# Window attention, forward and backward: six 64-row products per window pair as four 64 by 64 tiles of the PE array, with compact probabilities and a new step order

## Chip, cores, metric

One NeuronCore of one Trainium2 chip. The metric is device time of one execution in microseconds (us). PE is the engine of the matrix products, DVE the vector engine, ACT the scalar engine.

## The reference

The input is a 256 x 256 image of 384 channels, cut into 1024 windows of 8 x 8 = 64 tokens. Each window has single-head attention over its own tokens; the kernel computes the output and the gradients of x, wqkv and wo.

```python
qkv = xw @ wqkv                                  # xw: (1024, 64, 384)
p = softmax(einsum('bqc,bkc->bqk', q, k) * C ** -0.5)
o = einsum('bqk,bkc->bqc', p, v) @ wo
# ... and the vector-Jacobian product of all of it with grad_out
```

## The kernel before

Weights are multiplied together first, so that per token only projections by four 384 x 384 matrices remain. One body of the main loop handles four window pairs ("quad", t = 0..3); a pair fills the 128 partitions with two windows of 64 tokens. The body runs 128 times. Per pair, six products of the 64 x 64 probability matrix P, or of its gradient S, with token tensors of 384 columns are needed: the output, two inputs of the weight gradients (U, W), and three that accumulate into the gradient of x. P and S of the two windows stood on the diagonal of 128 x 128 matrices that were zeroed once, so that each product was one full-array product, half of it zeros.

```python
# softmax, step 3 (step 5 is alike for pd and S): one DVE operation per window, 64 partitions each
for w, h in halves:
    nc.vector.tensor_tensor(out=Pb[h, :, h], in0=ex[h, :, :], in1=ri[h, :]..., op=ALU.mult)

def turn(st, kind):            # PT, ST: 128 x 128 transposes, 512-column copy
    for t in range(QUAD):
        nc.tensor.transpose(pt[:, t, :], src[:, t, :], ident[:])
    nc.vector.tensor_copy(out=dst[:], in_=pt[:])

def attend(st, t, part):       # one 128-row product per part, three in part 3; ps_at has 2 buffers
    if part == 0:    matmul(pa, lhsT=PT[:, t, :], rhs=uq[:, t, :]);  ACT copies to osb; DMA out
    elif part == 1:  matmul(pa, lhsT=Pb[:, t, :], rhs=dq[:, t, :]);  DVE copies to Wq
    elif part == 2:  matmul(pa, lhsT=ST[:, t, :], rhs=xq[:, t, :]);  ACT copies to Uq
    else:            # Pb*zq + Sb*yq + ST*vq;                        ACT copies to dsb; DMA out

def step(a, b):                # a: this quad, b: the one before it
    A(project, 0, 0); B(0, 0); A(project, 0, 1); B(0, 1); A(project, 0, 2); B(0, 2); ...  # parts one by one
    filler(4); A(scores); A(soft, 0); ...
    # ... [cut: soft 1 to 5 between uv products and the other parts of B]
    for t in range(QUAD):
        A(yz_tok, t, 0); filler(2); A(yz_tok, t, 1); filler(2)   # token transposes, DVE copies yq, zq
    A(turn, 1); filler(2)
```

In the names, xq and dq are the tokens of x and grad_out; uq and vq are x times two of the four matrices, yq and zq the transposed projections by the other two. The softmax goes through mx (maximum), sh (shifted scores), ex, rs and ri (sum and its reciprocal) to P; pr, D and pd lead on to S.

A filler is one 384-column product of the weight gradient; twelve make a group, which DVE then adds to GF_acc. PE, DVE and ACT run in the order written here.

## Time and profile before

| | before |
|---|---|
| time, median of three runs | 2829.28 us (2827.99 to 2836.85) |
| mean body, from the first to the last score maximum | 21.54 us |
| PE / DVE / ACT busy | 88% / 70% / 49% |
| projections to scores ("stage 1"), softmax ("stage 2"), token transposes ("stage 3") of the body below | 6.68 / 10.13 / 4.69 us |

The page of the profile gives the busy time of each engine. PE records overlap, so 88% does not mean that the array streams for 88% of the time.

```profile
span 2827.3 us, 50549 instructions
PE 2485.4 (88%) x18814; PEld 1474.1 (52%) x18814; DVE 1976.6 (70%) x4899; ACT 1379.3 (49%) x2957; POOL 549.2 (19%) x1036
```

The chain of waits of the kernel before, one body. Columns: start (us), share of the chain (us), engine, output and line, number of instructions.

```profile
1422.04 0.65 PE pj L147 x3
1422.69 0.16 PE pa L243
...
1427.94 0.76 PE sd L161 x24
1428.70 0.02 issue
1428.72 0.43 DVE mx L174
...
1432.96 0.42 DVE P_bd_233 L192
1433.38 0.03 issue
1433.41 0.43 DVE P_bd_233 L192
...
1437.49 0.56 DVE Wq L249
1438.05 0.33 DVE PT L233
...
1438.85 0.28 DVE yq L225
...
1443.54 0.65 PE pj L147 x3
```

From 1422.04 to the first score maximum (mx, 1428.72) the chain lies on PE. From there to the first token copy (yq, 1438.85) it lies on DVE but for one visit to PE of 0.7 us. From there to the next body's first projection (1443.54) it is mostly on PE again. These three stretches are the stages of this text. Two groups of instructions that the change replaces (busy us, mean ns of one; then idle time before them):

```profile
L248 PE MATMUL pa<-dq,P_bd_225 128*128 128x384 bf16 x172 | 56.1, 326 | 0.0
L192 DVE TENSOR_TENSOR P_bd_225<-ex,ri 64x256 bf16<-64x256 f32 x86 | 36.1, 420 | 2.9
```

There is such a group for each of the three block-diagonal buffers.

### The profile page before, as it was taken

The numbers are of one execution on the slowest core, as the hardware profiler recorded it, in microseconds if no ns is written. First come the engines' busy times: TensorE is split into PE (matmuls) and PEld (weight loads), VectorE is DVE, ScalarE is ACT, GpSimd is POOL, SyncE is SP. The second block draws the span as 40 slices with busy tenths as digits, with TensorE's granted clock in tenths as the row PEclk, the third lists the DMA queues.
The fourth block names the chain that finished last, engine by engine and source line by source line (L and its number), as shares of the span: only waits on it lengthen the run. The fifth ranks groups of instructions, "written<-read, shape, count | busy, mean of one in ns | idle before, by whom it ended". The sixth has DMA issues, their size and how long they took to land.

```text
span 2827.3 us, 50549 instructions
## 1 busy us (share of the span) xinstructions
PE 2485.4 (88%) x18814; PEld 1474.1 (52%) x18814; DVE 1976.6 (70%) x4899; ACT 1379.3 (49%) x2957; POOL 549.2 (19%) x1036
## 2 busy tenths in 40 slices
PE   6888988888898888889888988888898888889887
PEld 3455555555555555555555555555555555555554
DVE  5677677767767776776777677677767776776774
ACT  3554554455455445545544554554454445545552
POOL 2121122112111211211221121112111211221110
PEclk9999999999999999999999999999999999999999
DMA  6444444455444444445554444444445544444441
GB/s 154 92 112 103 110 106 110 111 115 122 113 110 106 111 103 110 112 105 116 117 118 107 111 108 107 107 108 108 106 116 113 122 109 111 106 110 105 110 93 41
DMA packets 599863, 307.74 MB, mean 109 GB/s; under 512 B 434240, under 2 KB 582464, under 8 KB 599616
## 3 DMA queue, kind: packets, MB, share of 16 engines
q1 hardware_dynamic: 550064, 203.49, 34.2%
q0 software_dynamic: 49152, 100.73, 12.9%
q8 instruction: 147, 2.41, 0.3%
q14 instruction: 100, 0.82, 0.1%
q10 hardware_dynamic: 400, 0.29, 0.0%
HBM read 101.84 MB, written 101.84 MB: 72 GB/s over the span
## 4 chain that ended last, share of the span: by engine, by line
PE 51%; DVE 43%; issue 3%; DMA 2%; ACT 1%; SPq 0%; ACTq 0%; DVEq 0%
PE pj L147 18%; PE pw L271 13%; DVE uq L218 9%; PE pt L224 5%; DVE sh L180 4%; DVE mx L174 4%; PE pj L216 3%; PE sd L161 3%; DVE pr L197 3%; DVE pd L204 3%; DVE yq L225 3%; DVE GF_acc L274 3%; DVE Wq L249 2%; DVE D L199 2%; DMA out_dram<-osb 2%
## 5 line engine op out<-in xcount | busy, mean ns | idle before, releaser
L259 POOL DMA_DIRECT2D out_dram<-dsb x512 | 275.3, 538 | 2205.6 <-ACT dsb L258 2170.9
L150 ACT CAST yz<-pj 128x512 bf16<-128x512 f32 x384 | 227.1, 592 | 843.1 <-PE pj L147 843.1
L216 PEld LDWEIGHTS <-xT 128*128 128x128 bf16 x3072 | 299.2, 97 | 368.8 <-issue 200.4
L249 DVE CAST Wq<-pa 128x384 bf16<-128x384 f32 x512 | 283.4, 554 | 272.8 <-PE pa L248 268.8
L216 PE MATMUL pj<-B_sb,xT 128*128 128x384 bf16 x1536 | 333.3, 325 | 98.9 <-ACT vq L218 72.6
L271 PE MATMUL pw<-Wq,xq 128*128 128x384 bf16 x1536 | 364.2, 326 | 47.6 <-DVE GF_acc L274 47.6
L252 ACT CAST Uq<-pa 128x384 bf16<-128x384 f32 x512 | 245.7, 480 | 315.3 <-PE pa L251 315.3
L271 PE MATMUL pw<-Uq,xq 128*128 128x384 bf16 x1536 | 359.9, 326 | 24.9 <-DVE GF_acc L274 24.9
L216 PE MATMUL pj<-AT_sb,xT 128*128 128x384 bf16 x1536 | 334.6, 327 | 35.3 <-DVE uq L218 35.3
L271 PEld LDWEIGHTS <-xq 128*128 128x128 bf16 x3072 | 258.5, 98 | 142.3 <-issue 89.9
L147 PE MATMUL pj<-dT,BT_sb 128*128 128x512 bf16 x1152 | 316.0, 384 | 6.2 <-DMA dT<-dq 6.2
L218 DVE CAST uq<-pj 128x384 bf16<-128x384 f32 x512 | 284.5, 556 | 43.5 <-PE pj L216 35.5
L147 PE MATMUL pj<-xT,A_sb 128*128 128x512 bf16 x1152 | 311.3, 379 | 0.0
L245 ACT CAST osb<-pa 128x384 bf16<-128x384 f32 x512 | 246.8, 482 | 92.3 <-DMA out_dram<-osb 52.2
L258 ACT CAST dsb<-pa 128x384 bf16<-128x384 f32 x512 | 244.9, 478 | 73.5 <-PE pa L256 61.1
L132 POOL DMA_DIRECT2D dq<-in_grad_out_dram x512 | 270.6, 542 | 37.8 <-PE pt L232 26.1
L218 ACT CAST vq<-pj 128x384 bf16<-128x384 f32 x512 | 244.0, 477 | 57.2 <-PE pj L216 54.7
L224 PE MATMUL pt<-ident,zc 128*128 128x128 bf16 x1536 | 169.9, 220 | 95.5 <-DVE PT L233 94.8
L225 DVE COPY yq<-pt 128x384 bf16<-128x384 bf16 x512 | 182.1, 356 | 102.6 <-PE pt L224 85.3
L153 ACT CAST yz<-pj 128x512 bf16<-128x512 f32 x384 | 229.9, 599 | 16.4 <-PE pj L147 0.7
L151 DVE COPY zc<-yz 128x512 bf16<-128x512 bf16 x384 | 112.9, 294 | 177.8 <-ACT yz L150 177.7
L224 PEld LDWEIGHTS <-zc 128*128 128x128 bf16 x1536 | 129.1, 98 | 178.7 <-issue 121.3
(107 smaller groups left out, 3558.8 us busy)
## 6 DMA issues: line engine op xcount, KB each, us to landing
xq<-in_x_dram SPq DMA_DIRECT2D x512, 96.0 KB, 2.5
dq<-in_grad_out_dram POOLq DMA_DIRECT2D x512, 96.0 KB, 2.5
out_dram<-osb SPq DMA_DIRECT2D x512, 96.0 KB, 2.2
out_dram<-dsb POOLq DMA_DIRECT2D x512, 96.0 KB, 2.1
xT<-xq SPq DMA_TRANSPOSE x128, 4.7
dT<-dq SPq DMA_TRANSPOSE x128, 3.7
w_sb<-in_wqkv_dram SPq DMA_DIRECT2D x1, 864.0 KB, 5.7
out_dram<-dw_sb SPq DMA_DIRECT2D x1, 864.0 KB, 3.8
```

Of the source, the lines that this page charges most:

```text
L132: nc.gpsimd.dma_start(out=dq[:, t, :], in_=dram_tile(grad_out, bp, t0 + t))
L147: nc.tensor.matmul(pj[:].rearrange("p t w k -> p (t w k)"), lhsT=wgt[:, m, mo * P:(mo + 1) * P], rhs=src[:, :, m, :], start=(m == 0), stop ...
L216: nc.tensor.matmul(pj[:], lhsT=st["xT"][:, t, m, :], rhs=wgt[:, m, :], start=(m == 0), stop=(m == CK - 1))
L218: cp(out=dst[:, t, :], in_=pj[:])
L224: nc.tensor.transpose(pt[:, m, :], src[:, m, :, :].rearrange("p w k -> p (w k)"), ident[:])
L225: nc.vector.tensor_copy(out=dst[:, t, :].rearrange("p (m c) -> p m c", m=CK), in_=pt[:])
L245: nc.scalar.copy(out=osb[:], in_=pa[:])
L249: nc.vector.tensor_copy(out=st["Wq"][:, t, :], in_=pa[:])
L252: nc.scalar.copy(out=st["Uq"][:, t, :], in_=pa[:])
L258: nc.scalar.copy(out=dsb[:], in_=pa[:])
L259: nc.gpsimd.dma_start(out=dram_tile(out_1, bp, t0 + t), in_=dsb[:])
L271: nc.tensor.matmul(pw[:], lhsT=st["xq"][:, t, ma * P:(ma + 1) * P], rhs=st["UW"[f] + "q"][:, t, :], start=(i == 0), stop=(i == n - 1))
```

## The change

Intent: use the array's four 64 x 64 quadrants for four products of 64 rows at once. Two products are issued together, one placed "straight" (rows low to low, high to high) and one "crossed", so that the four tiles never write the same PSUM partitions of the same bank. P and S are then stored compactly, 64 columns instead of 128, which also makes one DVE operation out of two. All attention of a pair is issued in one piece, four PSUM buffers hold its results, the transposes share the two buffers of the projections, and the step order is new.

```diff
-            for w, h in halves:
-                nc.vector.tensor_tensor(out=Pb[h, :, h], in0=ex[h, :, :], in1=ri[h, :]..., op=ALU.mult)
+            nc.vector.tensor_tensor(out=Pb[:], in0=ex[:], in1=over_k(ri[:]), op=ALU.mult)
 # ... [cut: the same for pd and S]
+            for h in (LO, HI):
+                nc.tensor.transpose(pt[h, t, :], src[h, t, :], ident[h, h])
 # ... [cut]
+        def both(straight, crossed):
+            for h, o, (dst, lhs, rhs, first, last) in ((LO, LO, straight), (LO, HI, crossed), (HI, LO, crossed),
+                                                       (HI, HI, straight)):
+                nc.tensor.matmul(dst[o, :], lhsT=st[lhs][h, t, :], rhs=st[rhs][h, t, :], start=first, stop=last)
+        both((po, "PT", "uq", True, True), (pd, "Pb", "zq", True, False))
+        ...                                                # ACT copies po
+        both((pu, "ST", "xq", True, True), (pd, "Sb", "yq", False, False))
+        both((pw, "Pb", "dq", True, True), (pd, "ST", "vq", False, True))
+        ...                                                # DVE copies pw, ACT copies pu and pd
 # ... [cut] the new order of one body:
+        A(project, 0, 0); A(project, 0, 1); B(0); A(project, 0, 2); A(project, 1, 0); B(1)
+        A(project, 1, 1); A(project, 1, 2); filler(8); A(scores); A(soft, 0); A(soft, 1); filler(4)
+        A(uv, 0, 0); A(uv, 0, 1); A(soft, 2); A(uv, 1, 0); A(uv, 1, 1); A(soft, 3); B(2)
+        A(uv, 2, 0); A(uv, 2, 1); A(soft, 4); A(uv, 3, 0); A(uv, 3, 1); filler(4); A(soft, 5)
+        for t in range(QUAD): A(yz_tok, t, 0); filler(1); A(yz_tok, t, 1); filler(1)
+        B(3); A(turn, 0); A(turn, 1)
```

More of the change, by code (lines that the diff above doesn't have):

```diff
@@ L60 @@
     ps_pj = ctx.enter_context(tc.tile_pool(name="ps_pj", bufs=2, space=bass.MemoryType.PSUM))
-    ps_tr = ctx.enter_context(tc.tile_pool(name="ps_tr", bufs=2, space=bass.MemoryType.PSUM))
     ps_sd = ctx.enter_context(tc.tile_pool(name="ps_sd", bufs=1, space=bass.MemoryType.PSUM))
-    ps_at = ctx.enter_context(tc.tile_pool(name="ps_at", bufs=2, space=bass.MemoryType.PSUM))
+    ps_at = ctx.enter_context(tc.tile_pool(name="ps_at", bufs=4, space=bass.MemoryType.PSUM))
     ps_dw = ctx.enter_context(tc.tile_pool(name="ps_dw", bufs=1, space=bass.MemoryType.PSUM))
@@ L75 @@
     for jm in range(JK):
-        pt = ps_tr.tile([P, C], BF16, tag="tr")
+        pt = ps_pj.tile([P, C], BF16, tag="pj")
         for m in range(CK):
@@ L81 @@
     for mo in range(CK):
-        pt = ps_tr.tile([P, C], BF16, tag="tr")
+        pt = ps_pj.tile([P, C], BF16, tag="pj")
         for m in range(CK):
@@ L108 @@
     nc.vector.memset(GF_acc[:], 0.0)
-    NBD = 3
-    P_bds = []
-    S_bds = []
-    for i in range(NBD):
-        pb = const.tile([P, QUAD, P], BF16, name=f"P_bd{i}")
-        nc.gpsimd.memset(pb[:], 0.0)
-        P_bds.append(pb)
-        sb = const.tile([P, QUAD, P], BF16, name=f"S_bd{i}")
-        nc.gpsimd.memset(sb[:], 0.0)
-        S_bds.append(sb)
     def dram_tile(ap, bp, t):
         return ap[0, 2 * WIN * bp:2 * WIN * (bp + 1), WIN * t:WIN * (t + 1), :]
-    halves = ((0, slice(0, WT)), (1, slice(WT, P)))
+    LO, HI = slice(0, WT), slice(WT, P)
     def load(st):
         bp, t0 = st["at"]
-        st["xq"] = xq = grp.tile([P, QUAD, C], BF16, tag="xq", name="xq", bufs=2 * GQ + 2)
+        st["xq"] = xq = grp.tile([P, QUAD, C], BF16, tag="xq", name="xq", bufs=2 * GQ + 3)
         st["dq"] = dq = qp.tile([P, QUAD, C], BF16, tag="dq", name="dq", bufs=4)
@@ L164, in scores, with over_k @@
                                      start=(m == 0), stop=(m == CK - 1))
+    def over_k(ap, n=P):
+        return ap.unsqueeze(2).broadcast_to([n, QUAD, WT])
     def soft(st, step):
@@ L168, in soft @@
         if step == 0:
-            st["Pb"] = P_bds[st["i"] % NBD]
-            st["Sb"] = S_bds[st["i"] % NBD]
             st["mx"] = mx = sm.tile([P, QUAD], F32, tag="mx", name="mx")
-            for w, h in halves:
-                o = slice(WT, P) if w == 0 else slice(0, WT)
-                nc.vector.tensor_reduce(out=mx[o, :], in_=sd[o, :, w, :], axis=AX.X, op=ALU.max)
+            for w, h in ((0, HI), (1, LO)):
+                nc.vector.tensor_reduce(out=mx[h, :], in_=sd[h, :, w, :], axis=AX.X, op=ALU.max)
         elif step == 1:
@@ L177, in soft @@
             st["sh"] = sh = sm.tile([P, QUAD, WT], F32, tag="sh", name="sh")
-            for w, h in halves:
-                o = slice(WT, P) if w == 0 else slice(0, WT)
-                nc.vector.tensor_tensor(out=sh[h, :, :], in0=sd[o, :, w, :],
-                                        in1=mx[o, :].unsqueeze(2).broadcast_to([WT, QUAD, WT]), op=ALU.subtract)
+            for w, h, o in ((0, HI, LO), (1, LO, HI)):
+                nc.vector.tensor_tensor(out=sh[o, :, :], in0=sd[h, :, w, :], in1=over_k(mx[h, :], WT),
+                                        op=ALU.subtract)
         elif step == 2:
@@ L185, in soft @@
         elif step == 3:
-            ex, Pb = st["ex"], st["Pb"]
+            ex = st["ex"]
             rs = sm.tile([P, QUAD], F32, tag="rs")
@@ L190, in soft @@
             nc.vector.reciprocal(out=ri[:], in_=rs[:])
-            for w, h in halves:
-                nc.vector.tensor_tensor(out=Pb[h, :, h], in0=ex[h, :, :],
-                                        in1=ri[h, :].unsqueeze(2).broadcast_to([WT, QUAD, WT]), op=ALU.mult)
+            st["Pb"] = Pb = qp.tile([P, QUAD, WT], BF16, tag="Pb", name="Pb")
+            nc.vector.tensor_tensor(out=Pb[:], in0=ex[:], in1=over_k(ri[:]), op=ALU.mult)
         elif step == 4:
             st["pr"] = pr = sm.tile([P, QUAD, WT], F32, tag="pr", name="pr")
-            for w, h in halves:
-                nc.vector.tensor_tensor(out=pr[h, :, :], in0=sd[h, :, w, :], in1=st["Pb"][h, :, h], op=ALU.mult)
+            for w, h in ((0, LO), (1, HI)):
+                nc.vector.tensor_tensor(out=pr[h, :, :], in0=sd[h, :, w, :], in1=st["Pb"][h, :, :], op=ALU.mult)
             st["D"] = D = sm.tile([P, QUAD], F32, tag="D", name="D")
@@ L200, in soft @@
         else:
-            Pb, Sb, D, pr = st["Pb"], st["Sb"], st["D"], st["pr"]
             pd = sm.tile([P, QUAD, WT], F32, tag="pd")
-            for w, h in halves:
-                nc.vector.tensor_tensor(out=pd[h, :, :], in0=Pb[h, :, h],
-                                        in1=D[h, :].unsqueeze(2).broadcast_to([WT, QUAD, WT]), op=ALU.mult)
-            for w, h in halves:
-                nc.vector.tensor_tensor(out=Sb[h, :, h], in0=pr[h, :, :], in1=pd[h, :, :], op=ALU.subtract)
+            nc.vector.tensor_tensor(out=pd[:], in0=st["Pb"][:], in1=over_k(st["D"][:]), op=ALU.mult)
+            st["Sb"] = Sb = qp.tile([P, QUAD, WT], BF16, tag="Sb", name="Sb")
+            nc.vector.tensor_tensor(out=Sb[:], in0=st["pr"][:], in1=pd[:], op=ALU.subtract)
     def uv(st, t, part):
@@ L221, in yz_tok @@
         src, dst = ((st["yz"][:, :, t, 1:3, :], st["yq"]), (st["zc"][:, :, t, :, :], st["zq"]))[part]
-        pt = ps_tr.tile([P, CK, P], BF16, tag="tr")
+        pt = ps_pj.tile([P, CK, P], BF16, tag="pj")
         for m in range(CK):
@@ L228, in turn @@
         src, n = ((st["Pb"], "PT"), (st["Sb"], "ST"))[kind]
-        st[n] = dst = qp.tile([P, QUAD, P], BF16, tag=n, name=n)
-        pt = ps_tr.tile([P, QUAD, P], BF16, tag="tr")
+        st[n] = dst = qp.tile([P, QUAD, WT], BF16, tag=n, name=n)
+        pt = ps_pj.tile([P, QUAD, WT], BF16, tag="pj")
         for t in range(QUAD):
-            nc.tensor.transpose(pt[:, t, :], src[:, t, :], ident[:])
+            for h in (LO, HI):
+                nc.tensor.transpose(pt[h, t, :], src[h, t, :], ident[h, h])
@@ L233, in turn, with attend @@
         nc.vector.tensor_copy(out=dst[:], in_=pt[:])
-    def attend(st, t, part):
+    def attend(st, t):
         bp, t0 = st["at"]
-        if t == 0 and part == 0:
+        if t == 0:
             st["Uq"] = grp.tile([P, QUAD, C], BF16, tag="Uq", name="Uq")
             st["Wq"] = grp.tile([P, QUAD, C], BF16, tag="Wq", name="Wq")
-        Pb, Sb, PT, ST = st["Pb"], st["Sb"], st["PT"], st["ST"]
-        pa = ps_at.tile([P, C], F32, tag="at")
-        if part == 0:
-            nc.tensor.matmul(pa[:], lhsT=PT[:, t, :], rhs=st["uq"][:, t, :], start=True, stop=True)
-            osb = ob.tile([P, C], BF16, tag="o")
-            nc.scalar.copy(out=osb[:], in_=pa[:])
-            nc.sync.dma_start(out=dram_tile(out_0, bp, t0 + t), in_=osb[:])
-        elif part == 1:
-            nc.tensor.matmul(pa[:], lhsT=Pb[:, t, :], rhs=st["dq"][:, t, :], start=True, stop=True)
-            nc.vector.tensor_copy(out=st["Wq"][:, t, :], in_=pa[:])
-        elif part == 2:
-            nc.tensor.matmul(pa[:], lhsT=ST[:, t, :], rhs=st["xq"][:, t, :], start=True, stop=True)
-            nc.scalar.copy(out=st["Uq"][:, t, :], in_=pa[:])
-        else:
-            nc.tensor.matmul(pa[:], lhsT=Pb[:, t, :], rhs=st["zq"][:, t, :], start=True, stop=False)
-            nc.tensor.matmul(pa[:], lhsT=Sb[:, t, :], rhs=st["yq"][:, t, :], start=False, stop=False)
-            nc.tensor.matmul(pa[:], lhsT=ST[:, t, :], rhs=st["vq"][:, t, :], start=False, stop=True)
-            dsb = ob.tile([P, C], BF16, tag="d")
-            nc.scalar.copy(out=dsb[:], in_=pa[:])
-            nc.gpsimd.dma_start(out=dram_tile(out_1, bp, t0 + t), in_=dsb[:])
@@ new lines, in attend @@
+        po = ps_at.tile([P, C], F32, tag="at", name="po")
+        pd = ps_at.tile([P, C], F32, tag="at", name="pd")
+        pu = ps_at.tile([P, C], F32, tag="at", name="pu")
+        pw = ps_at.tile([P, C], F32, tag="at", name="pw")
+        def both(straight, crossed):
+            for h, o, (dst, lhs, rhs, first, last) in ((LO, LO, straight), (LO, HI, crossed), (HI, LO, crossed),
+                                                       (HI, HI, straight)):
+                nc.tensor.matmul(dst[o, :], lhsT=st[lhs][h, t, :], rhs=st[rhs][h, t, :], start=first, stop=last)
@@ new lines, in attend @@
+        both((po, "PT", "uq", True, True), (pd, "Pb", "zq", True, False))
+        osb = ob.tile([P, C], BF16, tag="o")
+        nc.scalar.copy(out=osb[:], in_=po[:])
+        nc.sync.dma_start(out=dram_tile(out_0, bp, t0 + t), in_=osb[:])
+        both((pu, "ST", "xq", True, True), (pd, "Sb", "yq", False, False))
+        nc.scalar.copy(out=st["Uq"][:, t, :], in_=pu[:])
+        both((pw, "Pb", "dq", True, True), (pd, "ST", "vq", False, True))
+        nc.vector.tensor_copy(out=st["Wq"][:, t, :], in_=pw[:])
@@ L261 @@
+        dsb = ob.tile([P, C], BF16, tag="d")
+        nc.scalar.copy(out=dsb[:], in_=pd[:])
+        for h, w in ((LO, 1), (HI, 0)):
+            nc.gpsimd.dma_start(out=dram_tile(out_1, bp, t0 + t)[WIN * w:WIN * (w + 1)], in_=dsb[h, :])
     fill = []
@@ L290, in step @@
         A = (lambda f, *r: f(a, *r)) if a is not None else (lambda f, *r: None)
-        B = (lambda t, p: attend(b, t, p)) if b is not None else (lambda t, p: None)
+        B = (lambda t: attend(b, t)) if b is not None else (lambda t: None)
         A(project, 0, 0)
-        B(0, 0)
         A(project, 0, 1)
-        B(0, 1)
+        B(0)
         A(project, 0, 2)
-        B(0, 2)
         A(project, 1, 0)
-        B(0, 3)
+        B(1)
         A(project, 1, 1)
-        B(1, 0)
         A(project, 1, 2)
-        B(1, 1)
-        filler(4)
+        filler(8)
         A(scores)
         A(soft, 0)
-        B(1, 2)
-        filler(2)
-        B(1, 3)
         A(soft, 1)
+        filler(4)
         A(uv, 0, 0)
-        B(2, 0)
+        A(uv, 0, 1)
         A(soft, 2)
-        A(uv, 0, 1)
-        B(2, 1)
         A(uv, 1, 0)
+        A(uv, 1, 1)
         A(soft, 3)
-        B(2, 2)
-        A(uv, 1, 1)
-        B(2, 3)
+        B(2)
+        A(uv, 2, 0)
+        A(uv, 2, 1)
         A(soft, 4)
-        A(uv, 2, 0)
-        B(3, 0)
-        A(uv, 2, 1)
+        A(uv, 3, 0)
+        A(uv, 3, 1)
+        filler(4)
         A(soft, 5)
-        B(3, 1)
-        A(turn, 0)
-        A(uv, 3, 0)
-        B(3, 2)
-        A(uv, 3, 1)
-        B(3, 3)
         for t in range(QUAD):
             A(yz_tok, t, 0)
-            filler(2)
+            filler(1)
             A(yz_tok, t, 1)
-            filler(2)
+            filler(1)
+        B(3)
+        A(turn, 0)
         A(turn, 1)
-        filler(2)
     quads = [(bp, t0) for bp in range(NBP) for t0 in range(0, NT, QUAD)]
@@ L363 @@
         for mb in range(CK):
-            pt = ps_tr.tile([P, C], BF16, tag="tr")
+            pt = ps_pj.tile([P, C], BF16, tag="pj")
             for ma in range(CK):
```

## The prediction

> **What bounds the kernel now.** The loop body (four window pairs) runs 128 times; in the chain of waits two bodies follow each other at 1400.4 and 1422.0 us, a period of 21.6 us. The page gives PE 88%, DVE 70%, ACT 49%, but PE's records overlap: in the timeline products follow each other every 0.163 us (384 columns) or 0.216 us (512), so PE streams about 18 us per body. The chain of waits shows three stages. (1) Projection to scores, 6.8 us, PE-bound. (2) Softmax and its gradient, 10.0 to 10.1 us: from 1428.7 to 1438.8 us the chain lies on DVE almost without a gap. (3) Token transposes with fillers, 4.7 us, PE-bound. A faster PE alone would not shorten stage 2.
>
> **What the change does, per body.**
> - PE: 24 attention products (3.9 us) become 48 of 64x64x384. If four tiles run at once, that is 12 slots, about 2.0 us. The Trainium skill ("TensorE: Matmul & The Clock Gate", Part 3) says that packed tiles start about 4 ns apart; it says ("TensorEngine Tiling (Array Packing)", Tiling Modes) that a change of tiling mode drains the array. Four tiled sections mean eight changes; estimated from the 0.16 us by which a recorded 384-column product (0.327 us) outlasts its spacing, 1.2 to 1.6 us. So about 0.8 to 0.95 us per pair instead of 0.98: most of the PE gain is given back. The doubled transposes may cost 0.3 to 0.6 us more.
> - DVE: P, pd and S become one 128x256 operation each in place of two of 64x256 (0.42 us each): -1.26 us. PT and ST copies: -0.35 us. Together -1.6 of 15.4.
> - Moved: out of stage 2 go one Wq copy (0.55) and PT; a GF_acc addition (0.55) always falls into it. Eight fillers move before the scores, eight of the sixteen stay among the transposes, whose two PSUM buffers are now the projections'.
>
> **On the critical path, by stage** (my estimate). (1) 3.9 us projections + 1.7 tiled attention + 1.3 fillers + 0.76 scores + 0.2 = 7.9 to 8.1 us (ACT needs nearly the same). (2) DVE: 8.1 us against 10.05. (3) With fewer fillers the eight copies and their two-buffer handshake set the pace: 3.2 us, then GF_acc, Wq, PT and the last attention 1.5 to 1.6 us. Sum 20.7 to 21.0 against 21.6. So the gain comes mainly from DVE, not from the array: 0.6 to 1.2 us x 128 = 80 to 150 us.
>
> **Prediction: 2715 us, range 2600 to 2840; faster by over 2%: 0.70, within 2%: 0.18, slower: 0.12.**
>
> **What would show each step right or wrong.** P, pd, S groups each 128 records of 128x256 at about 0.42 us, DVE busy about 1780 us. Tiled products starting in near-simultaneous fours, groups 0.16 to 0.22 us apart; a gap of 0.1 to 0.2 us at each change between full and tiled. Stage 2 near 8 us on DVE; stage 3 on DVE rather than PE; stage 1 a microsecond longer. GF_acc no longer holding up PE's fillers (72 us before), ACT's osb no longer waiting for DMA.
>
> **What would make it wrong.** Tiles of one row half running one after another (group 0.33 us): pair 1.3 us, the stages on PE grow by 1.5 us, time 2800 to 2900. All four in turn: over 3000. Slow 64-column weight loads (over 50 ns, in series): the last transposes delay the next body. Cheap drains would bring 2620.

## The result, and the profile after

| | before | after |
|---|---|---|
| median (four runs each) | 2830.05 us | 2574.93 us (2573.89 to 2576.12) |
| ratio of fast runs | | 0.9095 (0.9079 to 0.9111) |
| mean body | 21.54 us | 19.64 us |
| stage 1 / 2 / 3 of one body | 6.68 / 10.13 / 4.69 us | 7.52 / 7.94 / 4.20 us |

All ratios here are the mean time of one kernel's fast runs over that of the other's of the same rounds, so not quite the ratio of the medians quoted. The time fell by 255 us; the prediction had 114 and a range that ended at 2600. The direction was right, the size was not.

```profile
span 2574.3 us, 59437 instructions
PE 2318.2 (90%) x22910; PEld 1259.7 (49%) x22910; DVE 1751.3 (68%) x4515; ACT 1295.4 (50%) x2957; POOL 862.0 (33%) x1542
```

The chain of waits of the kernel after, from one score maximum to the next (stage 2, stage 3, then stage 1 of the next body):

```profile
1401.19 0.43 DVE mx L162
...
1405.16 0.42 DVE Pb L179
1405.59 0.47 DVE Wq L241
...
1409.13 0.28 DVE yq L208
...
1412.06 0.46 DVE GF_acc L260
1412.52 0.55 DVE Wq L241
1413.08 0.21 DVE PT L217
1413.29 0.04 issue
1413.33 1.46 PE pj L135 x6
1414.78 0.28 PE po L232
...
1415.07 0.15 PE pu L232
...
1415.39 1.40 PE pj L135 x6
...
1418.81 1.30 PE pw L257 x8
1420.11 0.71 PE sd L149 x24
1420.82 0.02 issue
1420.85 0.43 DVE mx L162
```

Stage 2 is 2.2 us shorter and still on DVE. Stage 1 is 0.8 us longer: it now has twelve attention products and eight fillers where it had eight and four. A whole attention pair takes 0.61 us there (1414.78 to 1415.39), and the six projection products that follow take 1.40 us, where the same six without a change of mode (from full-array products to tiles or back) before them take 1.29 (in a run below). The groups that answer to those above:

```profile
L232 PE MATMUL pw<-dq,Pb 64*64 64x384 bf16 x1024 | 170.7, 323 | 0.0
L179 DVE TENSOR_TENSOR Pb<-ex,ri 128x256 bf16<-128x256 f32 x128 | 54.3, 424 | 4.4
```

Four tiles do run at once. PE's timeline of the kernel after, one attention pair between two full-array products:

```profile
1404.41 0.32 PE L199 MATMUL pj<-AT_sb,xT 128*128 128x384 bf16 x1
1404.66 0.35 PE L232 MATMUL po<-uq,PT 64*64 64x384 bf16 x1
1404.67 0.35 PE L232 MATMUL pd<-zq,Pb 64*64 64x384 bf16 x2
1404.67 0.35 PE L232 MATMUL po<-uq,PT 64*64 64x384 bf16 x1
1404.85 0.32 PE L232 MATMUL pu<-xq,ST 64*64 64x384 bf16 x1
...
1405.01 0.32 PE L232 MATMUL pw<-dq,Pb 64*64 64x384 bf16 x1
...
1405.28 0.34 PE L199 MATMUL pj<-B_sb,xT 128*128 128x384 bf16 x1
```

The four starts of a group lie within 0.01 us, as the Trainium skill has it ("TensorE: Matmul & The Clock Gate", Part 3: about 4 ns per tile). The groups follow each other after 0.16 to 0.19 us. Full-array products of 384 columns follow each other after 0.163 us, so the first tile starts 0.09 us late (0.25 after the product before it), and the next full product 0.11 us late (0.27 after the last group).

### The profile page after: what moved, and what is told of

It is laid out like the page before. It is cut to its first block, busy times and chain, and to the rows that moved or that the text cites. A ratio compares the mean times of both kernels' runs of the same rounds, so it can differ in the third digit from the quotient of the medians.

```text
span 2574.3 us, 59437 instructions
## 1 busy us (share of the span) xinstructions
PE 2318.2 (90%) x22910; PEld 1259.7 (49%) x22910; DVE 1751.3 (68%) x4515; ACT 1295.4 (50%) x2957; POOL 862.0 (33%) x1542
## 3 DMA queue, kind: packets, MB, share of 16 engines
q8 instruction: 179, 2.93, 0.5%
## 4 chain that ended last, share of the span: by engine, by line
DVE 49%; PE 47%; issue 2%; ACT 0%; DMA 0%; SPq 0%; ACTq 0%
PE pj L135 21%; DVE uq L201 10%; PE pw L257 10%; PE pt L207 6%; DVE GF_acc L260 5%; DVE Wq L241 5%; DVE sh L167 4%; DVE mx L162 4%; DVE pr L183 4%; PE sd L149 4%; DVE yq L208 3%; PE po L232 3%; DVE Sb L190 2%; DVE Pb L179 2%; DVE D L185 2%
## 5 line engine op out<-in xcount | busy, mean ns | idle before, releaser
L245 POOL DMA_DIRECT2D out_dram<-dsb x1024 | 586.4, 577 | 1056.1 <-ACT dsb L243 1032.0
L236 ACT CAST osb<-po 128x384 bf16<-128x384 f32 x512 | 255.0, 498 | 508.2 <-PE po L232 500.2
L135 PE MATMUL pj<-dT,BT_sb 128*128 128x512 bf16 x1152 | 293.4, 381 | 80.2 <-DVE PT L217 79.9
L257 PEld LDWEIGHTS <-xq 128*128 128x128 bf16 x3072 | 291.0, 98 | 137.2 <-issue 6.3
L162 DVE TENSOR_REDUCE mx<-sd 64x4 f32<-64x256 f32 x256 | 108.2, 422 | 361.7 <-PE sd L149 357.7
L257 PE MATMUL pw<-Uq,xq 128*128 128x384 bf16 x1536 | 339.1, 326 | 1.9 <-DVE GF_acc L260 1.9
L241 DVE CAST Wq<-pw 128x384 bf16<-128x384 f32 x512 | 283.8, 554 | 18.4 <-PE pw L232 3.6
L243 ACT CAST dsb<-pd 128x384 bf16<-128x384 f32 x512 | 266.9, 521 | 0.0
L239 ACT CAST Uq<-pu 128x384 bf16<-128x384 f32 x512 | 260.5, 509 | 0.0
L207 PE MATMUL pt<-ident,yz 128*128 128x128 bf16 x1536 | 168.1, 217 | 49.1 <-DVE yq L208 46.9
```

Of the source, the lines that this page charges most:

```text
L135: nc.tensor.matmul(pj[:].rearrange("p t w k -> p (t w k)"), lhsT=wgt[:, m, mo * P:(mo + 1) * P], rhs=src[:, :, m, :], start=(m == 0), stop ...
L207: nc.tensor.transpose(pt[:, m, :], src[:, m, :, :].rearrange("p w k -> p (w k)"), ident[:])
L236: nc.scalar.copy(out=osb[:], in_=po[:])
L239: nc.scalar.copy(out=st["Uq"][:, t, :], in_=pu[:])
L241: nc.vector.tensor_copy(out=st["Wq"][:, t, :], in_=pw[:])
L243: nc.scalar.copy(out=dsb[:], in_=pd[:])
```

## The experiments

All results below were correct. The kernel before had medians of 2830 to 2833 us. Theory A is the one formed from the traces: PE's time counts in stages 1 and 3, DVE's in stage 2, and the tiled products cost less than predicted.

### Two tiles at once in place of four

```diff
-        def both(straight, crossed): ...
+        def both(*products):
+            for dst, lhs, rhs, first, last in products:
+                for h in (LO, HI):
+                    nc.tensor.matmul(dst[h, :], lhsT=st[lhs][h, t, :], rhs=st[rhs][h, t, :], start=first, stop=last)
```

> The kernel after, but each product's two 64x64 tiles both placed straight (rows low to low, high to high), one product after the other: two tiles at once in place of four, six slots per window pair in place of three; the compact vector operations and the order stay. Theory A (the array gain is on the critical path in the stages that PE and its releases pace): each tiled section grows by 3 x 0.16 = 0.49 us; two sections lie in stage 1, one before the end of stage 3, one is hidden under DVE in stage 2, so about +1.4 us a body, 2700 to 2770 us. Theory B (the prediction: the gain is mainly DVE's): within 25 us of 2575.

Measured: 2792.92 us, ratio 0.9861 (0.9846 to 0.9875); mean body 21.35 us, 1.71 more than after. Stages 8.47 / 8.42 / 4.48 us. The chain of waits of this run, a pair in stage 1:

```profile
1405.28 0.28 PE po L232 x2
1405.56 0.16 PE pd L232 x2
...
1406.21 0.16 PE pd L232 x2
1406.37 1.40 PE pj L135 x6
```

Six slots, 1.09 us, where four tiles need 0.61. Stage 1 grew by 0.95 us, two pairs' worth. Theory B is out: the four-way placement is worth something on the critical path; without it, 218 of the 255 us are lost. But the time is above theory A's range too, which was not right in everything: the pair in stage 2, which should have hidden under DVE, cost 0.48 us. That came up again below.

### The DVE operations split again

```diff
-            nc.vector.tensor_tensor(out=Pb[:], in0=ex[:], in1=over_k(ri[:]), op=ALU.mult)
+            for h in (LO, HI):
+                nc.vector.tensor_tensor(out=Pb[h, :, :], in0=ex[h, :, :], in1=over_k(ri[h, :], WT), op=ALU.mult)
 # and the same for pd and Sb
```

> The kernel after, but P, pd and S again in two operations of 64x256 each. Theory A and B agree that stage 2 is DVE-bound: three more operations of 0.43 us, +1.3 us a body, 2720 to 2750 us. Theory C (order and PSUM buffers alone make the gain): within 25 us of 2575.

Measured: 2802.94 us, ratio 0.9892 (0.9875 to 0.9908); mean body 21.41 us, +1.77. Stages 7.52 / 9.55 / 4.33: nearly all of it is stage 2. Theory C is out. The time is above the range expected: the loss is more than the 1.3 us that three operations cost. The chain of waits of this run shows why, against 1405.16 to 1405.59 of the kernel after:

```profile
1402.68 0.42 DVE Pb L180
1403.11 0.03 issue
1403.14 0.56 DVE Wq L245
```

After the whole operation, Wq takes 0.47 us of the chain; after the split one it takes 0.03 + 0.56. The same loss shows at pr, which reads P, and at yq, which follows S: some 0.1 us at each of the three places. The Trainium skill ("Perfetto Trace Analysis", Per-instruction lifecycle) says that a record of DVE lasts until the write is acknowledged, while the next operation may begin its prefetch before that; the 0.08 us by which successive records overlap in after (Pb ends at 1405.59, Wq starts at 1405.51) agree with it. In after the same loss shows where half-partition operations remain: sh, which writes the upper 64 partitions, ends at 1402.98, and GF_acc starts only at 1403.01. Why the overlap is lost with split operations was not tried.

### The arithmetic of before in the new order

Block-diagonal P and S, full-array products and full transposes of before, put into the order and the PSUM buffers of after. Two block-diagonal sets had to do instead of three, for lack of SBUF.

```diff
+        def both(*products):
+            for dst, lhs, rhs, first, last in products:
+                nc.tensor.matmul(dst[:], lhsT=st[lhs][:, t, :], rhs=st[rhs][:, t, :], start=first, stop=last)
 # soft and turn as in the kernel before
```

> Block diagonal operands, full-array products, full transposes and split vector operations as before, in the order and with the PSUM buffers of after (two block-diagonal sets in place of three, to fit). Theory A: both savings are undone, +1.4 - 0.6 (no mode changes) + 1.3 + 0.1 us a body, 2790 to 2880 us, so the order alone gains nothing. Theory C: 2575 to 2650 us.

Measured: 2898.86 us, ratio 1.0234 (1.0219 to 1.0249); a little above the range expected. Stages 8.03 / 9.56 / 4.58 us. The order, with the PSUM buffers and the two sets that came with it, loses 66 us. In this run a pair takes six slots of 0.163 us, 0.98 in all, and the projections after it 1.29 us. So the tiled pair of after costs 0.61 + 0.11 = 0.72 us against 0.98: it saves 0.26 us, about half of the 0.49 us that three slots are. Twice this makes stage 1's difference from after, 0.51 us.

### The arithmetic of after in the old order, first try

```diff
+        A(project, 0, 0); A(project, 0, 1); A(project, 0, 2); B(0); A(project, 1, 0); ...
+        A(soft, 0); B(1); filler(2); ... A(uv, 0, 1); B(2); ... A(soft, 5); B(3); A(turn, 0); A(uv, 3, 0); ...
 # fillers 4, 2, eight times 2, 2 as before
```

> Tiled products and compact vector operations as after, but in an order close to that of before (one whole attention pair where the four parts of it were centred, fillers and transposes of P as before). Theory A: stage 2 8.6 us, stage 1 6.6, stage 3 4.6: a body of 19.8 us, 2560 to 2680 us. Theory C: above 2780 us.

Measured: 2895.11 us, ratio 1.0221 (1.0203 to 1.0238), a clear miss. It was not a clean test. PE waited for DVE 0.92 and then 0.81 us late in stage 2, and in the 4 us after that the granted clock was 0.59, with weight-gradient products 0.32 us apart instead of 0.16; the mean granted clock was 0.964 (0.997 in after). The second of these waits was for the PT copy, with which the projections now share their two PSUM buffers. So this hybrid added waits of its own, and the lower clock came on top.

### The arithmetic of after in exactly the old order

Each group of four tiles stands alone, where a part of the pair stood.

```diff
+        if part == 0:    both((po, "PT", "uq", ...), (st["pd"], "Pb", "zq", ...)); ...
+        elif part == 2:  both((pu, "ST", "xq", ...), (st["pd"], "Sb", "yq", ...)); ...
+        elif part == 3:  both((pw, "Pb", "dq", ...), (st["pd"], "ST", "vq", ...)); ...
 # step() as in the kernel before
```

> Tiled products and compact vector operations of after in exactly the step order and filler places of before, each group of four tiles on its own where a part of the pair stood (twelve tiled sections a body and two for the transposes; no long idle time of PE, unlike the hybrid tried before, whose PE clock fell to half after a wait). Theory A: four sections of 0.39 us in stage 1, 7.0 us; stage 2 8.3 us by DVE; stage 3 4.7 us: 20.1 us a body, 2600 to 2690 us.

Measured: 2874.6 us, ratio 1.0153 (1.0138 to 1.0168), granted clock 0.998. Stages 7.15 / 10.20 / 4.66 us: stages 1 and 3 as expected, stage 2 missed by 1.9 us. The expectation had forgotten that the second Wq copy now falls into stage 2 (0.56 us), and that DVE would wait for PE there: 0.74 us before a uq copy and 0.60 before a Wq copy in the body looked at. PE's timeline of this run shows what a lone group costs:

```profile
1402.92 0.82 PE L135 MATMUL pj<-xT,A_sb 128*128 128x512 bf16 x3
1403.68 0.35 PE L228 MATMUL pw<-dq,Pb 64*64 64x384 bf16 x1
...
1403.96 0.82 PE L135 MATMUL pj<-xT,A_sb 128*128 128x512 bf16 x3
```

From one projection to the next are 1.04 us; three projection products alone take 0.65 us. The group takes 0.39 us, and the two full-array products that it replaces take 0.33. A group on its own, entered and left, is slower than what it replaces; three in a row are faster.

PE also waited here for the shared buffers: the transposes of P stood 0.57 us until ACT's vq copy was done (1414.36 us).

The four corners together:

| median, us | old order | new order |
|---|---|---|
| arithmetic of before | 2830 to 2833 | 2899 |
| arithmetic of after | 2875 | 2575 |

Only the corner of before has the PSUM buffers of before. The other three have those of after, where the transposes share the projections' buffers. How much of a step from before is order and how much is buffers was not separated.

### More changes of mode with the same work, in stage 1

```diff
+        if t < 2: filler(1)        # between the first and second group, and between the second and third
-        filler(8)
+        filler(4)
```

> The kernel after, with four of the eight fillers that stand before the scores put one each into the two gaps between the three groups of four tiles, in the first and the second attention pair: the same products, eight more mode changes a body, in the PE-bound stage 1. From the trace of after one section costs 0.12 us on entry and 0.11 on exit, so theory A: 4 gaps x 0.23 = +0.92 us a body, 2670 to 2720 us. If a change cost what the prediction supposed (0.15 to 0.2 us): 2730 to 2780 us. If the 0.61 us section is dominated by something else than mode changes: under 2620 us.

Measured: 2706.29 us, ratio 0.9557 (0.9541 to 0.9573); mean body 20.68 us, +1.04, stage 1 8.58 us, +1.06. Of this, 0.15 us is the scores, 0.86 us in the chain instead of 0.71, as fewer fillers stand between the last projection and them; the rest, 0.91 us over eight changes, is 0.11 us per change. The prediction had 0.15 to 0.2.

### More changes of mode in stage 2, twice

```diff
+        if t == 2: filler(2)       # in both gaps of the third pair
         A(uv, 3, 1)
-        filler(4)
```

> The kernel after, with the four fillers that stand before the last softmax step put two each into the two gaps of the third attention pair, in stage 2: four more mode changes a body, which would be +59 us if PE's time counted there. Theory A (DVE sets stage 2): within 20 us of 2575.

Measured: 2713.32 us, ratio 0.9581 (0.9567 to 0.9596); stage 2 9.05 us, +1.11. A clear miss: PE does not have that slack. In the kernel after, the source of the third Wq copy was complete 0.2 us before DVE came to it (1405.34 against 1405.51), and DVE works in order. Fillers and changes ahead of it, 1.1 us, stop DVE. To separate the two, the fillers were then taken from those that stood earlier:

```diff
         A(soft, 1)
-        filler(4)
```

> The kernel after, with the gaps of the third pair filled by the four fillers that stood before the first uv products instead of four that came later, so that no more work than before stands ahead of the third Wq copy, only four mode changes (0.5 us). In after the copy's source was ready about 0.25 us before DVE came to it. Theory A (the loss of 138 us with the later fillers came mostly from 0.65 us of fillers put ahead of that copy): +0.2 to +0.5 us a body, 2600 to 2640 us. If mode changes in this stage cost 1 us for some other reason: 2690 us or more.

Measured: 2660.12 us, ratio 0.9395 (0.9379 to 0.9411); mean body 20.30 us, +0.66, stage 2 8.64 us. It is less than with the later fillers, but more than expected. In this order the GF_acc addition comes directly after the gaps and waits for them as well, so the time of the run is no clean measure of four changes. Its trace gives their price all the same: the three groups of that pair start at 1407.85, 1408.56 and 1409.28 us, 0.72 us apart, where a group and two fillers stream for 0.49 (3 x 0.163). That leaves 0.23 us for two changes, 0.11 us each as in stage 1. What both runs and the one with two tiles show is that stage 2 of after has next to no room on PE ahead of the third Wq copy, although its chain runs on DVE.

### Moving DVE copies to ACT

The chain of after says that the next body waits for GF_acc, Wq and PT on DVE.

```diff
-        nc.vector.tensor_copy(out=st["Wq"][:, t, :], in_=pw[:])
+        (nc.scalar.copy if t == 3 else nc.vector.tensor_copy)(out=st["Wq"][:, t, :], in_=pw[:])
```

> The kernel after, with only the last Wq copy of a body (0.55 us) moved from DVE to ACT, which stands idle there. In the chain of after the next body's first projection waits for GF_acc, Wq, PT on DVE in turn. Theory A (this chain on DVE sets the end of stage 3): PT comes 0.5 us earlier, 2500 to 2530 us. Rival (PE's tiled pair and transposes set it, as the prediction feared): within 15 us of 2575.

Measured: 2524.42 us, ratio 0.8919 (0.8906 to 0.8932). Stage 3 is 3.81 us, 0.39 less, as theory A had it; PT now waits for the transposes on PE. Next, the copies of t = 2 and 3, of both Wq and uq:

```diff
+        (nc.scalar.copy if t >= 2 else nc.vector.tensor_copy)(out=st["Wq"][:, t, :], in_=pw[:])
+        if t >= 2: cp = nc.scalar.copy     # uq
```

> The kernel after, with the third and fourth of both the Wq and the uq copies on ACT: 1.5 us of DVE work leave stage 2 and 0.55 us stage 3. The runs so far say that PE has next to no slack in stage 2, so not all of it will show: PE needs about 6 us there and the copies now queue on ACT. Theory A: stage 2 6.7 to 7.2 us, 2360 to 2440 us. If stage 2 is held by PE alone: 2500 to 2530 us, as with the last Wq copy alone.

Measured: 2543.95 us, ratio 0.8987 (0.8972 to 0.9002), slower than moving one copy: a miss. The chain of waits of this run in stage 2:

```profile
1405.81 0.38 ACT Wq L243
1406.19 0.38 ACT dsb L245
1406.57 0.39 ACT uq L203
1406.96 0.04 issue
1407.01 1.14 PE pj L199 x6
```

The third uq copy stands behind four evacuations on ACT, and PE waits 0.79 us for the projection buffer that it frees. The chain has left DVE. With GF_acc also taken out of stage 2, by skipping eight fillers once at the start:

```diff
-        filler(8)
+        if fill and not late: late.append(1)     # the first time only: no fillers here
+        else: filler(8)
```

> As the one before, with eight fillers skipped once at the start, so that all later GF_acc additions fall behind the eight fillers before the scores, where DVE idles, and into the middle of the token transposes, and none into stage 2. If DVE still sets stage 2: 0.4 us a body less than the one before, 40 to 60 us. If PE or ACT sets it by now: within 15 us of it.

Measured: 2607.88 us, ratio 0.9211 (0.9197 to 0.9225), 64 us worse again. Neither expectation allowed for that. In the middle of the token transposes GF_acc delays the copies that free the two shared buffers: the chain goes through yq, zq and GF_acc there before PE can go on. Last, only the fourth Wq and the fourth uq copy:

```diff
+        if t == 3: cp = nc.scalar.copy     # uq, beside the Wq copy of t == 3
```

> The kernel after with the last Wq copy and the last uq copy of a body on ACT, the third ones again on DVE. What failed with four copies was that the third uq copy stood behind the four evacuations of the third pair on ACT, so that PE waited 0.8 us for its projection buffer; the fourth stands behind nothing but vq. Theory A: DVE's stage 2 is 0.45 us shorter than in the run with the last Wq copy alone (2524 us) and PE can just follow: 2455 to 2490 us. If PE cannot follow any more: within 15 us of 2524.

Measured: 2481.04 us, ratio 0.8759 (0.8746 to 0.8772), as theory A expected, and the fastest kernel: 94 us below after. Stage 2 is 7.5 us.

## Why the prediction was wrong

The headline of 2715 us was 0.9 us a body less than before, which is the low end, 20.7 us, of its own sum. Against that end:

| term, us a body | predicted | measured in after | difference |
|---|---|---|---|
| stage 1: six projections | 3.9 | 3.9 | |
| stage 1: two tiled pairs, with entry and exit | 1.7 | 1.44 (2 x 0.72) | -0.26 |
| stage 1: fillers, scores, start | 1.3 + 0.76 + 0.2 | 1.30 + 0.71 + 0.19 | -0.06 |
| stage 1, as summed | 7.9 | 7.52 | -0.38 |
| stage 2 on DVE | 8.1 | 7.94 | -0.16 |
| stage 3: eight copies | 3.2 | 2.93 (1409.13 to 1412.06) | -0.27 |
| stage 3: GF_acc, Wq, PT, last pair | 1.5 | 1.27 (1412.06 to 1413.33) | -0.23 |
| body | 20.7 | 19.66 | -1.04 |

1.04 us x 128 = 133 us, which is the miss of 140 us but for the ends of the program.

- **Right: what bounds the stages, and what the DVE part does.** Stage 2 shrank on DVE; P, pd and S became 128 records each of about 0.42 us; DVE's busy time fell to 1751 us (predicted about 1780); stage 1 grew; the waits of PE's fillers for GF_acc went from 72 to 4 us. Splitting the operations again gave back 228 of the 255 us.
- **Not borne out: "the gain comes mainly from DVE, not from the array".** The shares depend on the path taken. In the new order (2899 us, +66), tiles with the halved transposes and split operations bring 2803 us, -96, and compact DVE operations then 2575 us, -228. By way of the run with two tiles, compact operations with the halved transposes bring 2793 us, -106, and four tiles in place of two then 2575 us, -218. (Two tiles are no neutral stand-in for the full products: a pair of them costs 1.09 + 0.11 = 1.20 us against 0.98.) Undoing either part gives back most of the gain, so neither is the main one by itself. Placed in the old order, the same arithmetic loses 42 us against before.
- **Wrong in size: what tiles cost on PE.** The step that failed is "eight changes; estimated ... 1.2 to 1.6 us. So about 0.8 to 0.95 us per pair instead of 0.98: most of the PE gain is given back. The doubled transposes may cost 0.3 to 0.6 us more." A change was taken to cost as much as a product's record outlasts its spacing, 0.16 us. It cost 0.11 us, eight of them 0.9 us a body, a pair 0.72 us, and half of the gain was kept. The prediction's own alternative, "Cheap drains would bring 2620", had the direction. The eight tiled transposes of P take 0.12 us (from 1412.27 until those of S begin at 1412.39) where the four full ones took 0.22: they start in twos, 0.01 us apart, and the next two follow 0.02 us after them, so they save time instead of costing it. The cheaper pairs are 0.26 us of the miss in stage 1. Their price also bears on the tail of stage 3: the last pair and the transposes were ready before DVE, so that Wq followed GF_acc with no wait. The prediction had put this last pair on the path. With two tiles at once the tail did go through PE (1423.42 to 1424.37 us in the chain of that run), and stage 3 was 0.28 us longer.
- **Wrong in size as well: copies and DVE.** The two-buffer handshake of the token transposes was put at 3.2 us and took 2.93, and the list of stage 2 was 0.16 us too long; why, no run shows. Nor does stage 3 lie on DVE alone, as the prediction had it: from 1409.45 to 1411.37 us its chain is on PE's transposes and fillers. All errors had the same sign, so they added up: 0.38 us in stage 1, 0.16 in stage 2 and 0.50 in stage 3.
- **Not said by the prediction, and shown by the runs:** the new order, with its buffers, is not a detail. With the old arithmetic it loses, and without it the new arithmetic loses. It puts three groups behind one another, which makes the tiles pay on PE; but the hybrid had whole pairs too and lost, so this is not all of it.

What stays open: why split DVE operations cost later ones 0.1 us of overlap each, and what the order does without the shared PSUM buffers.

## What to carry to other kernels

Price a 64 x 64 tiling by the section, not by the product: here entering and leaving cost 0.23 us against 0.16 us saved per group of four tiles, so one group alone loses and three in a row win. A compact layout that merges two half-partition vector operations can be worth about as much as the array time, where the chain runs on the vector engine: undone alone, the two lose 228 and 218 us here. And before moving copies to an idle engine, look at what stands ahead of them in that engine's order: moving two gained 94 us, moving four gained 31.

## What the Trainium skill lacked or had wrong

- "TensorEngine Tiling (Array Packing)", Tiling Modes, says that changing the tiling mode drains the array, but gives no price. Here it is about 0.11 us per change at full clock (0.91 us for eight), so that a lone group of four 64x64x384 tiles takes 0.39 us against 0.33 for two full-array products.
- "TensorE: Matmul & The Clock Gate", Part 3, says in its list of what overlaps that weight loads overlap with running matmuls only when the row group differs; the paragraph before that list, and Part 2 of the same page, name the background weight buffer as a second case. Here the loads of the second group, for all four tiles, begin 0.03 us after the first group's products (1404.69 against 1404.66 us), and the groups still follow each other after 0.16 to 0.19 us: the list is too narrow for this trace, and the second case agrees with it.
- Neither of these two pages has a figure for tiled transposes. Here eight 64 x 64 transposes of bf16 take 0.12 us, four 128 x 128 ones 0.22.
- "TensorE: Matmul & The Clock Gate", Part 1, ties the half clock to an idle window of about 3.4 us; it names short, frequent idle times as well, but without a figure. In the hybrid order the half clock came (mean granted clock 0.59 over 4 us) after two waits of only 0.92 and 0.81 us with three products between them, so an unbroken idle window is not needed.
